# State added on TensorE, the second product in plain fp32, four kb buffers, one decode lane and other TensorE times in the order's model

## The chip, the core and the metric

The kernel runs on one core of one Trainium2 chip. The metric is the device time of one execution in microseconds (us): the median of the runs, 1130.55 us before. A profiled execution gives the trace. Five engines matter: TensorE (PE; its weight loads are PEld), VectorE (DVE), ScalarE (ACT), GpSimd (POOL), and SyncE (SP), which here issues the DMA transfers. Each executes its own instructions in the order in which they were written, and waits at an instruction until what it needs is there.

## The reference

Three layers in a row, in fp32. First a recurrence over 768 steps for 32 pairs of batch and head, each with a 40 x 40 state:

```python
for t in range(S):
    y[:, :, t] = np.einsum('bhd,bhde->bhe', rt, state)
    Sa = np.einsum('bhde,bhe->bhd', state, at)
    state = state * wt[:, :, None, :] - np.einsum('bhd,bhe->bhde', Sa, bt) + np.einsum('bhd,bhe->bhde', vt, kt)
```

Its output, 3072 tokens of 320, goes through a first network (x @ w_in to 1024, h times softmax(h), layer norm times g_ln, @ w_out back to 320) and a second one (@ w_in to 2048, leaky rectifier with alpha, @ w_out to 320). The weights reach the kernel as 64-bit floats, two 32-bit words a value; the kernel turns each into fp32 itself, which is called decoding here.

## The kernel before, in words

**Stages.** The recurrence is done in 24 steps of 32 time steps, called slots (`slot(g)`, lines 1163 to 1210); two slots make a window of 64, four share one triangular inverse. A slot's products on TensorE, each with fp32 operands and results in PSUM: `px` (line 593, the old state and v against a), `pu` (608, the inverse applied), `pf` (633), `pst` (647, the update of the state), `pg` (462 and 686, the products within a chunk), `pss` (667, the new state turned), `py` (718, the output), `pt` (557, kb turned into one of the KBS buffers), and every fourth slot `pv` and `pn` (523, the inverse). They are small, 16 to 104 rows by 16 to 64 columns, and most write to two or four separate column strips of TensorE. Results are copied back to SBUF by ACT, or multiplied or added on the way by DVE: in `stage_st` (lines 640 to 659) DVE adds pst to the old state in VUS and writes the new one (line 652); before the next step ACT copies pss to KBS (671).

**First network.** Three slots behind, a slot's 128 tokens go through `mm1` (767, 16 products of 512 columns), `soft` (785 to 799), `tr1` (826, transposes; ACT casts the result to a short form lnh, line 831, DVE makes the remainder lnl, line 832), `mm2` (842 to 844: for each of 8 row blocks three products of 320 columns, high x high, high x low, low x high, in the reduced fp32r type) and `tr2` (858). x reaches mm1 through DRAM: SP stores Y to xd (751) and loads xt from it (752, 753). From slot 20 on there are no windows left to prepare. The last four groups of tokens are done in phase 2 (lines 1409 to 1414).

**Decode.** Two lanes (`advance`, lines 984 to 1013). A wide one does the first network's 11 pieces of 512 values per partition; a narrow one the second network's 44 pieces of 256, one at a time: SP loads the packed words into the only raw tile (line 923), DVE splits (884, 885), ACT converts (888, 889), DVE sets sign and low bits (892, 896), POOL multiplies (906), SP stores the result to DRAM (1029). The next load is asked for once line 896 of the piece before is done.

**Order.** The program is written out by hand-made planning, at build time. A clock `now` runs along TensorE's instructions: `pace(dt, n)` adds the modelled time of a product and the columns it counts for, `run(engine, cost, f)` the modelled times of the other engines. DVE's background work (scans, masks on a, kb, inverse, decode) is put in by `fill` in a fixed order of priority when the model says that DVE is free. Between the small products, `pace` and `until` take pieces of the first network from a queue, or products whose result nobody reads (`zero`, line 285; `busy`, line 325, in the first four slots), so that TensorE's modelled activity stays above a floor.

**Phase 2** (lines 1297 to 1437) is the second network: products ph (1330) and acc (1348 to 1350), leaky on DVE, casts on ACT and POOL.

Below, the functions that the change touches.

Of the kernel before, what the change touches and what calls it, by code (L numbers as in the profile page):

```python
# [18 lines left out]
D = 40  # L19
# [5 lines left out]
VS, NC, NL = 0, (2, 3, 3, 3), (3, 3, 3, 0)  # L25
# [3 lines left out]
YSV, XSV, YLV, DPV, VRV, W1V = 1, 1, 1, 0, 0, 1  # L29
# [9 lines left out]
WO, JW = 1, 0  # L39
# [6 lines left out]
def tile_kernel(ctx: ExitStack, tc: tile.TileContext, w_fm, a0_fm, a_fm, kb_fm, r_fm, v_fm, v_tm,  # L46
# [19 lines left out]
    lims = flp.tile([128, 2], F32, name="lims")  # L66
    s1 = flp.tile([128, 1], F32, name="s1")
    one = flp.tile([128, 1], F32, name="one")
    bad = flp.tile([1, 1], F32, name="bad")
    badi = flp.tile([1, 1], I32, name="badi")  # L70
    ebias = flp.tile([128, 1], F32, name="ebias")
    half = flp.tile([128, 1], F32, name="half")
    tiny = flp.tile([128, 1], F32, name="tiny")
# [12 lines left out]
    m2 = pool(pm, "m2", 2)  # L86
    b2 = pool(ctx, "b2", 2, side="right")
# [13 lines left out]
    wo1h = cm.tile([128, K1, DM], F32R, name="wo1h")  # L101
    wo1l = cm.tile([128, K1, DM], F32R, name="wo1l")
# [4 lines left out]
    KBP = [ca.tile([128, 1280], F32, name=f"KBS{i}") for i in range(3)]  # L107
# [5 lines left out]
    tri = ca.tile([128, 321], F32, name="tri")  # L113
# [54 lines left out]
    work = {"dec": [], "inv": [], "scan": [], "xs": [], "xm": []}  # L168
    ORDER = {"V": ("inv", "dec", "xm", "scan"), "P": ("xs",)}
    ring, wring, port = [], [], []  # L170
    gens, turns, joins, lanes = [], [], [], []
# [45 lines left out]
    def fill(e):  # L217
        while free[e] < now[0]:
            for s in ("dec",) * (st["slot"] % 4 < 3) + ORDER[e]:
                if work[s] and work[s][0][0]() <= now[0]:  # L220
                    ready, cost, f, done = work[s].pop(0)
                    t = run(e, cost, f, ready())
                    if done:
                        done(t)
                    break
            else:
                return

    def settle():
        if plain():  # L230
            return
        while events and events[0][0] <= now[0]:
            heapq.heappop(events)[2]()
        fill("V")
        fill("P")
        pump()
# [168 lines left out]
    def prep_window(w):  # L405

        for pe in range(2):
            steps = scan_steps(w, pe)
            for i, (cost, f) in enumerate(steps):
                work["scan"].append((lambda: max(at(("wt", w)), at(("yt", 2 * w - 7)) if w > 3 else 0.0), cost, f,  # L410
                                     put(("H", w)) if pe and i == len(steps) - 1 else None))
        for c in range(2):
            for e in range(2):
                work["xm" if XSV else "xs"].append((lambda g=2 * w + c: max(at(("H", w)), at(("a_in", g))) + LAT, (0.7 if XSV else 1.2,),
                                   lambda g=2 * w + c, e=e: mult_a(g, e, 0, 1),
                                   put(("xsh", 2 * w + c)) if e else None))

        def done(t):
            put(("kbf", w))(t)
            if w + 1 < NW:  # L420
                prep_load(w + 1)
                prep_window(w + 1)
        for pe in range(2):
            for i in range(2):
                work["scan"].append((lambda: at(("kb_in", w)), (0.71,), lambda pe=pe, i=i: mult_kb(w, pe, i, nc.vector),
                                     done if pe and i else None))
# [11 lines left out]
    def mult_a(g, e, *pes):  # L438
# [4 lines left out]
        (nc.vector if XSV or w < 2 and e in DA else nc.gpsimd).tensor_tensor(out=o, in0=o, in1=h, op=ALU.mult)  # L443
# [5 lines left out]
    def gen1(g, half):  # L449
# [8 lines left out]
        for p in range(half * 4, half * 4 + 4):  # L458
# [5 lines left out]
            pace(0.19, 188)  # L464
# [26 lines left out]
    def inverse(W):  # L491
# [10 lines left out]
        def step(s):  # L502
            sh = [128, 2, 15 - s, s]
            tmp = b1.tile([128, 256], F32, name="tmp")[:, 0:2 * s * (15 - s)]
# [12 lines left out]
        def low():  # L517
            nc.scalar.activation(out=VR[:, :, 31:15:-1], in_=VT, func=AF.Identity, scale=tri[:, 320:321])

        def units(p, lhsT, rhs, rows, ls):  # L520
            for l in ls:
# [3 lines left out]
                pace(0.042, 16)  # L525
# [24 lines left out]
    def trans(w, q):  # L550
# [4 lines left out]
        for i in range(4):  # L555
            pace(0.09, 150)
            nc.tensor.transpose(pt[:, i, :], kbf[:, q * 4 + i].rearrange("p c a t -> p (c a t)"), ident[0:104, 0:104])  # L557
        for c in range(2):
            k = KBS[(2 * w + c) % 3]
# [25 lines left out]
    def stage_x(g):  # L585
# [3 lines left out]
        for p in range(8):  # L589
# [5 lines left out]
            pace(0.15, 119)  # L595
# [4 lines left out]
    def stage_u(g):  # L600
# [4 lines left out]
        for p in range(8):  # L605
# [3 lines left out]
            pace(0.15, 20)  # L609
# [8 lines left out]
    def blank(p):  # L618
# [3 lines left out]
        note(0.02, 100)  # L622

    def stage_uf(g, pe):
# [4 lines left out]
        for p in range(8):  # L629
# [5 lines left out]
            pace(0.098, 24)  # L635
# [3 lines left out]

    def stage_st(g, pe):  # L640
        k, v, vn = KBS[g % 3], VUS[g % 2], VUS[(g + 1) % 2]
        until(("U", g, pe), ("kb", g))
        p_, bk = bank([128, 8, 40], "pst")
        for p in range(8):
            for e, o in EO:
                q, s = slice(64 * e, 64 * e + 64), pe * 8 + p
                nc.tensor.matmul(p_[o:o + 40, p, :], lhsT=k[q, 1 - e, s, :], rhs=v[q, e, s, :], start=True, stop=True)  # L647
            pace(0.104, 74)
        for e, o in EO:
            sl = slice(pe * 8, pe * 8 + 8)  # L650
            d = vn[o:o + 40, e, sl, :]
            t = run("V", 0.5, lambda d=d, o=o, e=e: nc.vector.tensor_tensor(  # L652
                out=d, in0=p_[o:o + 40], in1=v[o:o + 40, e, sl, :], op=ALU.add), now[0] + PL)
            ring[bk] = t + LAT
            if g % 4 == 3:
                rs = st[(g + 1) // 2]["rs"]
                t = run("V" if VRV else "P", (0.5 if VRV else 0.75,), lambda d=d, o=o: (nc.vector if VRV else nc.gpsimd).tensor_tensor(
# [3 lines left out]
    def stage_s(g, pe):  # L661
        kn, vn = KBS[(g + 1) % 3], VUS[(g + 1) % 2]
        until(("vus", g + 1, pe))
        p_, bk = bank([128, 8, 40], "pss")
        for p in range(8):
# [3 lines left out]
            pace(0.104, 74)  # L669
# [6 lines left out]
    def stage_g2(g, half):  # L676
# [5 lines left out]
        for p in range(half * 4, half * 4 + 4):  # L682
# [4 lines left out]
            pace(0.19, 188)  # L687
        if half == 0:
            return
        def masked(e, q, t):  # L690
            u = run("P", (1.3,), lambda: nc.gpsimd.tensor_tensor(
                out=y[q, e], in0=y[q, e], in1=mask[q].unsqueeze(1).to_broadcast([64, 16, 32]), op=ALU.mult), t)
            put(("ys", g, e))(u + LAT)
        for e in range(2 * YSV):
# [6 lines left out]
        for e in range(0 if YSV else 2):  # L701
            q = slice(64 * e, 64 * e + 64)
            for pe in range(2):
                t = run("A", 0.37, lambda e=e, q=q, pe=pe: nc.scalar.copy(
                    out=y[q, e, pe * 8:pe * 8 + 8], in_=pg[64 * pe:64 * pe + 64, :, e]), now[0] + PL)
            later(t + LAT, lambda e=e, q=q, t=t: masked(e, q, t + LAT))
        ring[bk] = t + LAT

    def stage_y(g):
        w, c = divmod(g, 2)  # L710
        k, y = KBS[g % 3], YS[g % 2]
# [3 lines left out]
        for s in range(16):  # L715
# [3 lines left out]
            pace(0.098, 114)  # L719
# [976 lines left out]
```

## Time and profile before

| what | before |
|---|---|
| median of 3 runs (lowest, highest) | 1130.55 us (1129.92, 1136.22) |
| profiled execution, its span | 1136.73 us, 1134.9 us |
| TensorE busy | 1022.4 us, 90% of the span, 19146 products |
| DVE, ACT, POOL busy | 697.2, 524.6, 290.6 us |
| mean granted clock of TensorE | 0.921 |
| first px of slot 0, of slot 4, of slot 20 | 37.9, 179.5, 658.7 us |

The table is read with care: a busy TensorE may run at 1.2 instead of 2.4 GHz, its fillers count as busy, and the ends of its products are modelled and overlap the next one's start, so that the start-to-start time of a row is the price of a product and not its length. "issue" in the chain is time in which an engine waited for nothing that the profile shows.

### The profile page before, as it was taken

How to read it: one execution, taken by the hardware profiler on the slowest of the kernel's cores; microseconds unless marked ns; L12 is line 12 of the kernel's file. 1: busy time of each engine (PE TensorE's matmuls, PEld its weight loads, DVE VectorE, ACT ScalarE, POOL GpSimd, SP SyncE). 2: the span in 40 equal slices, each digit the busy share in tenths (PEclk: the TensorE clock that was granted, in tenths of full speed). 3: DMA queues.
4: the chain of work that ended last, by engine and by line, in shares of the span. 5: the costliest groups of instructions: out<-in, count | busy, mean ns of one | idle time of the engine just before them, and what ended most of it. 6: DMA issues, size and time to landing. Idle time of an engine off the chain costs nothing.

```text
span 1134.9 us, 43057 instructions
## 1 busy us (share of the span) xinstructions
PE 1022.4 (90%) x19146; PEld 839.8 (74%) x19146; DVE 697.2 (61%) x1372; ACT 524.6 (46%) x1214; POOL 290.6 (26%) x358
## 2 busy tenths in 40 slices
PE   6788879899889879888888899989999999999997
PEld 2455555677677667777776778879899999999997
DVE  8778847787387857894796645555444444444443
ACT  1346434756376536763675467668612121212121
POOL 4401111213112121112111211234333333333332
PEclk8798888989979889986998889999999999999999
DMA  6623334245344333542544343246402020201010
GB/s 172 160 78 109 105 92 105 76 107 146 90 123 125 104 89 93 142 137 54 145 136 118 94 118 94 75 150 192 134 1 70 1 70 1 70 1 48 1 24 15
DMA packets 106757, 104.00 MB, mean 92 GB/s; under 512 B 38340, under 2 KB 85188, under 8 KB 106564
## 3 DMA queue, kind: packets, MB, share of 16 engines
q1 hardware_dynamic: 106564, 101.17, 32.5%
q8 instruction: 152, 2.49, 0.9%
q14 instruction: 41, 0.34, 0.1%
HBM read 75.71 MB, written 25.43 MB: 89 GB/s over the span
## 4 chain that ended last, share of the span: by engine, by line
PE 67%; DVE 14%; DMA 8%; issue 6%; ACT 4%; POOL 1%; SPq 0%; DVEq 0%; ACTq 0%; POOLq 0%
PE ph L1330 15%; PE h L767 7%; PE acc L1350 5%; PE acc L1349 5%; PE acc L1348 5%; PE busy L325 3%; PE pf L633 2%; DMA raw<-in_w_in_dram 2%; PE py L718 2%; PE pss L667 2%; DMA raw<-in_w_out_dram 2%; PE zero L285 2%; PE po L842 2%; PE pst L647 2%; DMA xd<-Y 2%
## 5 line engine op out<-in xcount | busy, mean ns | idle before, releaser
L802 DVE TENSOR_SCALAR gt<-ph,al 128x512 f32<-128x512 f32 (+1 forms) x112 | 75.5, 674 | 188.5 <-PE ph L1330 188.4
L1337 POOL TENSOR_TENSOR gll<-gt,gh 128x512 fp32r<-128x512 f32 (+1 forms) x112 | 129.2, 1154 | 225.5 <-ACT gh L1336 224.2
L1336 ACT CAST gh<-gt 128x512 fp32r<-128x512 f32 (+1 forms) x112 | 62.4, 558 | 249.5 <-DVE gt L803 215.3
L906 POOL TENSOR_TENSOR dec<-em 128x256 f32<-128x256 f32 x44 | 38.5, 876 | 250.4 <-DVE em L896 177.4
L767 PE MATMUL h<-w1h,xt 128*128 128x512 f32 x240 | 97.6, 466 | 1.4 <-ACT h L775 1.3
L1350 PE MATMUL acc<-w2h,gll 128*128 128x320 f32 x288 | 88.9, 309 | 0.0
L1349 PE MATMUL acc<-w2l,gh 128*128 128x320 f32 x288 | 88.9, 309 | 0.0
L1348 PE MATMUL acc<-w2h,gh 128*128 128x320 f32 x288 | 88.8, 308 | 0.0
L325 PE MATMUL busy<-busy 128*128 128x512 bf16 x234 | 70.2, 454 | 5.1 <-DVE busy L1243 3.8
L803 DVE SCALAR_TENSOR_TENSOR gt<-ph,gt 128x512 f32<-128x512 f32 (+1 forms) x112 | 68.8, 615 | 3.7
L842 PE MATMUL po<-wo1h,lnh 128*128 128x320 f32 x192 | 68.2, 355 | 1.2 <-ACT lnh L831 1.2
L767 PE MATMUL h<-w1l,xt 128*128 128x512 f32 x144 | 67.8, 471 | 0.0
L843 PE MATMUL po<-wo1l,lnh 128*128 128x320 f32 x192 | 63.5, 331 | 2.5 <-issue 2.5
L652 DVE TENSOR_TENSOR VUS<-pst,VUS 40x320 f32<-40x320 f32 x92 | 45.0, 489 | 32.9 <-PE pst L647 30.8
L844 PE MATMUL po<-wo1h,lnl 128*128 128x320 f32 x192 | 63.7, 332 | 1.3 <-issue 1.1
L577 POOL MEMSET YS<- 64x512 f32 x44 | 22.9, 521 | 141.3 <-PE py L718 140.1
L561 ACT COPY KBS<-pt 64x160 f32<-64x160 f32 x192 | 54.9, 286 | 9.1 <-PE pt L557 6.6
L1330 PE MATMUL ph<-w1h,w2h 128*128 128x512 f32 x180 | 58.7, 391 | 0.0
L671 ACT COPY KBS<-pss 40x320 f32<-40x320 f32 x92 | 38.6, 420 | 38.1 <-PE pss L667 36.9
L767 PEld LDWEIGHTS h<-w1h,xt 128*128 128x128 f32 x240 | 47.9, 213 | 10.4 <-ACT h L775 2.1
L1348 PEld LDWEIGHTS acc<-w2h,gh 128*128 128x128 f32 x288 | 54.1, 188 | 1.2
L1349 PEld LDWEIGHTS acc<-w2l,gh 128*128 128x128 f32 x288 | 54.1, 188 | 1.2
(197 smaller groups left out, 2556.1 us busy)
## 6 DMA issues: line engine op xcount, KB each, us to landing
kbf<-in_kb_fm_dram SPq DMA_DIRECT2D x24, 416.0 KB
x2d<-x SPq DMA_DIRECT2D x24, 320.0 KB
raw<-in_w_in_dram SPq DMA_DIRECT2D x24, 256.0 KB
xd<-Y SPq DMA_DIRECT2D x24, 256.0 KB
xt<-xd SPq DMA_DIRECT2D x12, 512.0 KB
raw<-in_w_out_dram SPq DMA_DIRECT2D x20, 256.0 KB
wt<-in_w_fm_dram SPq DMA_DIRECT2D x24, 211.7 KB
VUS<-in_v_tm_dram SPq DMA_DIRECT2D x48, 80.0 KB
```

The source lines that it names most:

```text
L325: nc.tensor.matmul(st["busy"], lhsT=busy[:, 0:128], rhs=busy, start=True, stop=True)
L767: nc.tensor.matmul(st["h"][:, ns], lhsT=l, rhs=r, start=j == 0, stop=j == len(ops) - 1)
L802: nc.vector.tensor_scalar(out=tmp, in0=h, scalar1=0.0, scalar2=al, op0=ALU.min, op1=ALU.mult)
L803: nc.vector.scalar_tensor_tensor(out=o, in0=h, scalar=0.0, in1=tmp, op0=ALU.max, op1=ALU.add)
L842: nc.tensor.matmul(po, lhsT=lh[:, k], rhs=wo1h[:, k], start=k == 0, stop=False)
L843: nc.tensor.matmul(po, lhsT=lh[:, k], rhs=wo1l[:, k], start=False, stop=False)
L844: nc.tensor.matmul(po, lhsT=ll[:, k], rhs=wo1h[:, k], start=False, stop=k == K1 - 1)
L1330: nc.tensor.matmul(p, lhsT=l, rhs=r, start=j == 0, stop=j == len(ops) - 1)
L1337: nc.gpsimd.tensor_tensor(out=gll, in0=t, in1=f32(gh), op=ALU.subtract)
L1348: nc.tensor.matmul(acc, lhsT=gh[:, cs], rhs=oh, start=f == 0, stop=False)
L1349: nc.tensor.matmul(acc, lhsT=gh[:, cs], rhs=ol, start=False, stop=False)
L1350: nc.tensor.matmul(acc, lhsT=gll[:, cs], rhs=oh, start=False, stop=f == K2 - 1)
```

## The change

- `stage_st`: a new function `stage_i` first multiplies the old state by the identity into the PSUM banks of pst, and pst is accumulated on top. DVE's add becomes an ACT copy.
- `tr1`, `mm2`: no split of the normed activations and of w_out; one product of plain fp32 per row block instead of three in fp32r.
- KBS has four buffers instead of three; the turns of kb may be placed at point 'a' of a slot instead of 'z'.
- Decode: one lane for both networks, up to two pieces begun and two loaded, with two raw tiles and two work tiles; all pieces up to 512 wide. The scaling of w_out by g_ln goes into the last multiplication. A piece of the second network is decoded into its own raw tile and stored from there.
- `fill`: another order of priority on DVE (inverse first; scan, a and kb ahead of decode once their window is within EARLY = 4 slots).
- Other times and columns in the model of the order for nearly every product; other numbers of pieces per slot.
- Some small tiles are merged or shortened.

```diff
-VS, NC, NL = 0, (2, 3, 3, 3), (3, 3, 3, 0)
+NC, NL = (1, 2, 2, 2), (2, 2, 2, 0)
+EARLY = 4
...
-    KBP = [ca.tile([128, 1280], F32, name=f"KBS{i}") for i in range(3)]
+    KBP = [ca.tile([128, 1280], F32, name=f"KBS{i}") for i in range(4)]
...
     def fill(e):
         while free[e] < now[0]:
-            for s in ("dec",) * (st["slot"] % 4 < 3) + ORDER[e]:
-                if work[s] and work[s][0][0]() <= now[0]:
-                    ready, cost, f, done = work[s].pop(0)
+            soon, passed = ("xm", "kb", "scan"), ()
+            for s in ("inv",) + ("xm", "kb", "scan", "dec", "xm", "kb", "scan"):
+                if work[s] and work[s][0][0]() <= now[0] and (s not in soon or s in passed or
+                                                              st["slot"] >= 2 * work[s][0][4] - EARLY):
+                    ready, cost, f, done, *_ = work[s].pop(0)
...
-            pace(0.19, 188)
+            pace(0.115, 256)
-                pace(0.042, 16)
+                pace(0.072, rows)
-            pace(0.15, 119)
+            pace(0.08, 140)
-            pace(0.15, 20)
+            pace(0.08, 40)
-        note(0.02, 100)
+        note(0.11 * p.shape[1] / 8, 8 * p.shape[1])
...
+    def stage_i(g):
+        v = VUS[g % 2]
+        until(("U", g, 0), ("U", g, 1))
+        st["ps", g] = []
+        for pe in range(2):
+            p_, bk = bank([128, 8, 40], "pst")
+            for e, o in EO:
+                nc.tensor.matmul(p_[o:o + 40], lhsT=ident[0:104 - 8 * e, o:o + 40],
+                                 rhs=v[0:104 - 8 * e, e, pe * 8:pe * 8 + 8, :],
+                                 start=True, stop=False, skip_group_check=True)
+                pace(0.28, 640)
+            st["ps", g].append((p_, bk))
     def stage_st(g, pe):
...
-                nc.tensor.matmul(p_[o:o + 40, p, :], lhsT=k[q, 1 - e, s, :], rhs=v[q, e, s, :], start=True, stop=True)
-            pace(0.104, 74)
+                nc.tensor.matmul(p_[o:o + 40, p, :], lhsT=k[q, 1 - e, s, :], rhs=v[q, e, s, :], start=False,
+                                 stop=p == 7, skip_group_check=True)
+            pace(0.08, 80)
...
-            t = run("V", 0.5, lambda d=d, o=o, e=e: nc.vector.tensor_tensor(
-                out=d, in0=p_[o:o + 40], in1=v[o:o + 40, e, sl, :], op=ALU.add), now[0] + PL)
+            t = run("A", 0.43, lambda d=d, o=o: nc.scalar.copy(out=d, in_=p_[o:o + 40]), now[0] + PL)
...
-        chain(now[0] + PL, [("A", 0.6, lambda: nc.scalar.copy(out=h, in_=pt)),
-                            ("V", 0.7, lambda: nc.vector.tensor_tensor(out=ll[:, 4 * j:4 * j + 4, :], in0=pt,
-                                                                       in1=f32(h), op=ALU.subtract))],
+        u = run("A", 0.6, lambda: nc.scalar.copy(out=st["ln", t][:, 4 * j:4 * j + 4, :], in_=pt), now[0] + PL)
...
-            nc.tensor.matmul(po, lhsT=lh[:, k], rhs=wo1h[:, k], start=k == 0, stop=False)
-            nc.tensor.matmul(po, lhsT=lh[:, k], rhs=wo1l[:, k], start=False, stop=False)
-            nc.tensor.matmul(po, lhsT=ll[:, k], rhs=wo1h[:, k], start=False, stop=k == K1 - 1)
+        nc.tensor.matmul(po, lhsT=st["ln", t][:, piece], rhs=wo1[:, piece], start=piece == 0, stop=piece == K1 - 1)
...
+    def piece(src, dst=None, scales=(), eng="V", end=lambda o: []):
         n = src.shape[1] * src.shape[2]
+        raw = rawp.tile([128, 1024], U32, name="raw")[:, 0:2 * n]
         nc.sync.dma_start(out=raw.rearrange("p (k n) -> p k n", k=src.shape[1]), in_=src.bitcast(U32))
         def steps():
+            em = emp.tile([128, 2, 512], I32, name="em")[:, :, 0:n]
+            o = raw[:, 0:n].bitcast(F32) if dst is None else dst
+            return decode_steps(raw, em[:, 0], em[:, 1], o, scales, eng) + end(o)
...
+    def over():
+        return next((i for i in range(lane["taken"]) if i not in lane["done"]), lane["taken"])
+    def pump():
+        while lane["tasks"] and lane["taken"] < over() + 2:
+            lane["next"].append((lane["tasks"].pop(0)(), now[0] + DMA))
+            lane["taken"] += 1
+        while lane["next"] and lane["due"] > 0 and lane["begun"] < over() + 2:
+            steps, t = lane["next"].pop(0)
...
-                turn(2 * W + 1, q, p(0, 'z'), p(1, 'b'))
+                turn(2 * W + 1, q, p(0, 'a'), p(1, 'b'))
...
-            q.append((0.0, 0, lambda: soft(t1), lambda: decoded(11)))
+            q.append((0.0, 0, lambda: soft(t1), lambda: 0.0))
...
-                q.append((0.4, 960, lambda p=p: mm2(t2, p),
-                          lambda p=p: max(at(("ln", t2, p // 4)), 0.0 if p else wfree())))
+                q.append((0.55, 960, lambda p=p: mm2(t2, p),
+                          lambda p=p: max(at(("ln", t2, p // 4)), 0.0 if p else wfree(),
+                                          decoded(6 + (p * DM + DM + 511) // 512))))
...
         if not fin:
+            stage_i(g)
             stage_st(g, 0)
             stage_st(g, 1)
...
-        if g == 2:
-            until(lambda: decoded(6))
         stage_y(g)
```

## Rows read from the trace of the kernel before

**Rows 1.** Busy time of each engine by stretch: us, busy (instructions), PEclk, DMA, GB/s.
```profile
core 0: us, PE busy (x) PEld busy (x) DVE busy (x) ACT busy (x) POOL busy (x), PEclk, DMA share, GB/s
38.00:180.00 142.00, 117.64 (x3336) 74.63 (x3339) 104.50 (x228) 59.83 (x143) 14.80 (x30) 0.85 0.38 101
180.00:659.00 479.00, 418.50 (x11356) 335.81 (x11349) 350.27 (x746) 279.82 (x687) 94.82 (x148) 0.89 0.42 113
659.00:746.00 87.00, 83.77 (x1949) 69.32 (x1936) 46.57 (x94) 61.71 (x143) 20.43 (x27) 0.97 0.35 92
746.00:810.00 64.00, 59.86 (x383) 55.35 (x382) 33.00 (x57) 47.53 (x98) 23.54 (x25) 0.96 0.57 187
810.00:1135.00 325.00, 316.90 (x1833) 290.74 (x1831) 130.64 (x197) 66.73 (x122) 115.92 (x97) 0.99 0.11 28
```

**Rows 2.** The chain of waits, shares by line: 38 to 180 us, then 180 to 659 us.
```profile
by line: PE busy L325 23.4%; issue 10.0%; PE pv L523 4.5%; PE pf L633 4.4%; PE pn L523 4.0%; DVE XS L482 3.8%; PE pst L647 3.3%; PE pss L667 3.0%; PE pu L608 2.9%; PE h L767 2.8%; DVE VUS L652 2.8%; DVE F L381 2.6%; PE py L718 2.6%; DVE tmp 
...
by line: PE h L767 10.5%; issue 7.7%; DMA raw<-in_w_in_dram 5.5%; DMA raw<-in_w_out_dram 5.2%; PE zero L285 4.5%; DMA xd<-Y 4.2%; PE pss L667 3.5%; PE py L718 3.4%; PE pf L633 3.3%; PE po L842 3.2%; PE ptr L826 2.9%; PE pn L523 2.7%; PE po 
```

**Rows 3.** The chain of waits, pieces from 588 to 622 us: start, us, what.
```profile
592.22 4.88 DMA xd<-Y
...
597.63 6.02 DMA raw<-in_w_in_dram
...
607.01 3.43 DMA raw<-in_w_in_dram
...
616.01 3.51 DMA raw<-in_w_in_dram
```

**Rows 4.** DVE's groups, 180 to 659 us: busy us, mean ns | idle before, releasers.
```profile
L652 DVE TENSOR_TENSOR VUS<-pst,VUS 40x320 f32<-40x320 f32 x64 | 31.3, 489 | 13.6 <-PE pst L647 12.1
...
L832 DVE TENSOR_TENSOR lnl<-ptr,lnh 128x512 fp32r<-128x512 f32 x32 | 21.5, 686 | 17.3 <-ACT lnh L831 17.0
...
L884 DVE TENSOR_SCALAR em<-raw 128x256 int32<-128x256 int32 x39 | 11.9, 306 | 35.0 <-DMA raw<-in_w_out_dram 20.2 <-DMA raw<-in_w_in_dram 14.5
```

**Rows 5.** TensorE's groups, 180 to 659 us, same columns.
```profile
L285 PE MATMUL zero<-D 104*128 104x512 bf16 x127 | 33.8, 396 | 1.9 <-DVE XS L482 1.9
...
L523 PE MATMUL pn<-VR,LMN 32*32 32x32 f32 x1024 | 13.3, 211 | 10.6 <-issue 10.6
L523 PE MATMUL pv<-VT,GR 16*32 16x16 f32 x1024 | 12.6, 192 | 5.9 <-issue 5.9
```

**Rows 6.** TensorE in order of time, around 212 and 616 us: start, us, what.
```profile
210.60 2.07 PE L462 MATMUL pg<-XS,kbf 104*32 104x64 f32 x128
212.65 0.28 PE L608 MATMUL pu<-XP,LMN 32*32 32x40 f32 x8
...
213.40 0.31 PE L842 MATMUL po<-wo1h,lnh 128*128 128x320 f32 x1
...
213.84 0.31 PE L842 MATMUL po<-wo1h,lnh 128*128 128x320 f32 x1
...
616.23 0.80 PE L593 MATMUL px<-VUS,XS 104*32 104x40 f32 x64
616.96 0.41 PE L842 MATMUL po<-wo1h,lnh 128*128 128x320 f32 x1
```

**Rows 7.** What SP's own queue waited for, 180 to 659 us: us, times, longest.
```profile
SPq L923 <- DVE em L896: 36.0, 20, 5.5
...
SPq L752 <- DMA xd<-Y: 25.6, 10, 3.4
```

**Rows 8.** ACT's copies of 40 x 320, 180 to 659 us.
```profile
L671 ACT COPY KBS<-pss 40x320 f32<-40x320 f32 x64 | 26.9, 420 | 19.0 <-PE pss L667 18.2
```

**Rows 9.** The chain of waits over the whole span, a store of a decoded piece.
```profile
253.15 3.95 DMA wd<-dec
```

**Rows 10.** TensorE's fillers, 38 to 180 us.
```profile
L325 PE MATMUL busy<-busy 128*128 128x512 bf16 x174 | 53.2, 457 | 3.8 <-DVE busy L1243 3.8
```

More of the change, by code (lines that the diff above doesn't have):

```diff
@@ L661, in stage_s @@
     def stage_s(g, pe):
-        kn, vn = KBS[(g + 1) % 3], VUS[(g + 1) % 2]
+        kn, vn = KBS[(g + 1) % 4], VUS[(g + 1) % 2]
         until(("vus", g + 1, pe))
@@ L686, in stage_g2 @@
                     nc.tensor.matmul(pg[o:o + 32, p], lhsT=vuf[:, s, i, :], rhs=y[0:104, :, s, :], start=True, stop=True)
-            pace(0.19, 188)
+            pace(0.115, 256)
         if half == 0:
             return
[L690 to L694, printed above, removed]
+        for e in range(2):
             q = slice(64 * e, 64 * e + 64)
@@ L700, in stage_g2 @@
             put(("ys", g, e))(t + LAT)
[L701 to L706, printed above, removed]
         ring[bk] = t + LAT
@@ L975, in chunk_out @@
-            return steps
-        return ([lambda j=j: chunk_in(j) for j in range(6)] +
-                [lambda c=c: chunk_out(*c) for c in cuts(K1 * DM, WO)])
-    def pump():
-        for lane in lanes:
-            advance(lane)
-    def advance(q):
-        i = q["taken"]
-        if q["tasks"] and not q["next"] and q["read"] and q["done"] >= (6 if i == 6 else i - 1):
-            q["next"] = q["tasks"].pop(0)(), now[0] + DMA
-            q["taken"] += 1
-        if q["due"] <= 0 or not q["next"] or q["busy"]:
-            return
-        q["busy"], q["read"] = True, False
-        q["due"] -= 1
-        get, t = q["next"]
-        q["next"] = None
-        s, end = get()
-        def read(u):
-            q["read"] = True
-            chain(u, s[-1:], over)
-        def over(u):
-            if q["wide"]:
-                q["busy"], q["free"] = False, u
-            chain(u, end, ended)
-        def ended(u):
-            q["done"] += 1
-            if q["wide"] and q["done"] == 6 and "moved" in st:
-                moved()
-            if not q["wide"]:
-                q["busy"], q["free"] = False, u
-        chain(max(t, q["free"]), s[:-1], read)
@@ L1170, in due @@
         def due(n):
[L1171 removed]
+            lane["due"] += n
         if g + 1 < NG:
@@ L1261, in phase1 @@
                 slot(g)
-            lanes[1]["due"] = 100
-            while events or any(q["busy"] or q["next"] or q["tasks"] for q in lanes) or any(work.values()):
+            lane["due"] = 100
+            while events or lane["next"] or lane["tasks"] or any(work.values()):
                 now[0] += 0.1
@@ L1587, in tile_kernel @@
             ms.enter_context(tc.manual_schedule(engines={mybir.EngineType.PE}))
-        for t in (w1_tasks(), w2_tasks()):
-            lanes.append({"tasks": t, "due": 0 if lanes else len(t), "next": None, "busy": False, "free": 0.0, "done": 0,
-                          "taken": 0, "read": True, "wide": not lanes})
+        lane["tasks"] = w1_tasks() + w2_tasks()
+        lane["due"] = 11
         phase1()
```

202 lines of the change are left out of this document (85 added, 117 removed).

## The prediction

> **What bounds the kernel now.** I read the busy table by stretch first. The last 325 us, the second network alone, keep TensorE busy for 316.90 us at 0.99 of its clock [rows 1]; no part of the change touches them, and I carry them over unchanged. The change lives in the recurrence, from 38 to 746 us, and in the 64 us behind it. In the middle stretch, 180 to 659 us (slots 4 to 19, 479/16 = 29.9 us a slot), no engine is full: DVE is busy for 350.27 us (73%), ACT for 279.82 (58%). TensorE shows 418.50 us (87%), but a good part of that is not needed work: 33.8 us are zero products that only keep its clock up [rows 5], and the granted clock is 0.89, that is, a fifth of the time at 1.2 GHz instead of 2.4, or up to 0.11 x 479 = 53 us of full clock. From 659 to 746 us TensorE really is full: 83.77 of 87 us, clock 0.97.
>
> So the middle is bound by waits, and the chain of waits says which. Of the chain from 180 to 659 us, 5.5% + 5.2% = 10.7% (51 us) are loads of packed weights into raw; 4.2% (20 us) are the store xd<-Y; 7.7% are issue [rows 2]. The reader should see how a weight decode that nothing needs soon can hold up everything: a load of 3.43 to 6.02 us lies on the chain [rows 3], DVE executes in its written order, and so the split of line 884 stands on DVE waiting for its load, for 35.0 us in all [rows 4], with the masks, Yt and lnl behind it, for which TensorE waits. In the first stretch, 38 to 180 us, 23.4% of the chain are fillers (busy), and DVE is busy for 104.50 of 142 us [rows 1, 2].
>
> **Plain fp32 second product.** It replaces three reduced-precision products of 320 columns, which start 213.84 - 213.40 = 0.44 us apart as a group, 0.147 each, by one fp32 product [rows 6]. Fp32 appears in the trace as two records for each product (64 records for the 32 products of a px). The lowest price is one pass per record, 2 x 0.147 = 0.29 us. For the other end, px needs 616.96 - 616.23 = 0.73 us for 64 records of 40 columns, 11.4 ns each; at the 0.46 ns a column of the 0.147 us product 40 columns would need 18 ns, so its four column strips run side by side. Then the 128 records (64 products of 64 columns, four at a time) of pg, 212.65 - 210.60 = 2.05 us, are 1024 columns, 2.0 ns each: 0.64 us for 320 columns. I take 0.60, because pg is the same kind of product. There are 192: 192 x (0.60 - 0.44) = +31 us of TensorE; the ends are 192 x (0.29 - 0.44) = -29 and 192 x (0.64 - 0.44) = +38.
>
> On this price the Trainium skill, page "FP8 and Floating Point Precision", section "TensorE Precision Notes", speaks against the change: true fp32 takes four passes through the array, not the two that a count of records suggests. By that rule an estimate from the row of 0.147 us is 192 x (4 x 0.147 - 0.44) = +28 us, by two passes it would be -29; the rate of pg agrees with the rule.
>
> What leaves DVE for it: 48 subtractions lnl, in the middle 21.5 us of work and 17.3 us in which DVE stood waiting for ACT ahead of them [rows 4].
>
> **State by an identity product.** Each of 46 calls gets two fp32 products of 320 columns, on different column strips: 0.60 us if they run side by side, as those of px do, 1.20 if not. I take 0.60: 46 x 0.60 = +28 us (upper end 55). They come behind the wait for U and in front of pst, so they lengthen that path by 1.2 us a slot; px, pss and py of the slot follow. In exchange 92 adds of 489 ns go from DVE to ACT [rows 4], where a copy of the same shape takes 420 ns [rows 8]: +38.6 us on ACT. ACT has 199 us free in the middle, but its queue is in order too: the new copies stand behind the two copies to VUF, and pss and the copies to KBS wait for them.
>
> **Decode in one lane, two buffers.** 44 pieces of 256 columns become 28 (16 of 512, 12 of 256), still 28 x up to four DVE instructions; the columns are the same, so I count DVE's decode time at nothing either way (work on DVE that has 27% free covers a difference). What counts is the load. Before, one raw tile serves: its load cannot be issued until line 896 of the piece before has read it, SP itself stands 36.0 us for that [rows 7], and the piece asked for next runs at once. Now two tiles exist, and a load is issued as soon as the piece two before has ended; with two pieces or one a slot that is about half a slot, 15 us, ahead of use, against the 6.02 us of the slowest load. I therefore let most of the 35.0 us on DVE go. Of the 51 us on the chain I credit 30: what is late next is xd<-Y with the SP queue, and TensorE itself.
>
> The price on SP: the decoded piece now lies in its own raw tile, so the next load into it waits until the store to wd has landed, 3.95 us [rows 9]. For 28 pieces that is some 28 x 4 = 112 us in which SP stands, and the loads of VUS, YS, VUF, wt and the xt loads stand behind it. SP waits 36.0 us for line 896 and 25.6 us for xd already [rows 7]. I cost this at nothing because those loads are issued a slot ahead; without that cover it is the second rival.
>
> **Four kb buffers, priorities, times in the model.** A fourth buffer lets the turns of kb be placed without waiting for the last y. No instruction is added. The order's model now charges a unit of pv and pn 0.072 us instead of 0.042, so it puts more of the large products between them. This matters: TensorE stands 10.6 + 5.9 = 16.5 us there for nothing but issue [rows 5]. I credit 14 of the clock's 53 and these 16.5 together; the ends are 0 and 40.
>
> **The sum**, against the profiled execution of 1136.7 us (span 1134.9 and 1.8 around it):
> - 38 to 180 us: 16 adds, 7.8 us, leave DVE, and the five pieces of w_out lose a scaling and a subtraction; the identities (4 x 1.2 us) lie inside the 53.2 us of fillers [rows 10]. -4.
> - 180 to 659 us: loads -30; adds and lnl, 84 us of DVE's work and standing [rows 4], mostly covered, -8; clock and issue -14; TensorE +16 x 1.2 = 19 and +128 x 0.16 = 20, of which I charge 16 because 33.8 us of zero products and 479 - 418.5 = 60.5 us of idle time can take the rest. -36.
> - 659 to 746 us: TensorE is full, so 3 x 1.2 + 32 x 0.16 = +9.
> - 746 to 810 us: 32 x 0.16 = +5, all on the path.
>
> Together -26: 1110.7 for an execution like the profiled one. The median of the runs is 1130.55, 6.2 below that; so I forecast 1130.55 - 26 = 1104.5, in round numbers **1105 us**, its own range 1085 to 1119.
>
> **The rivals.**
> 1. TensorE becomes the bound, and it is slower. Place: slots 4 to 19 and the full slots behind. None of the +39 us there finds cover, because the idle time sits ahead of products (behind ACT's copies, behind issue) where the order cannot put anything; the 14 of the full stretches come on top: 53. Of the loads only 20 are won: +33, **1163 us**. It decides once less than half of the added 2.4 us a slot replaces fillers or idle time. For it: a fully loaded TensorE from 659 us on. Against: 94 us of fillers and idle time in the middle. Chance 0.20.
> 2. SP's queue takes back what raw gave. The stores' landings hold SP, xd and xt arrive later, and the first network's products wait. If 8 of the 28 holds hit that path at 4 us each, 30 us are lost again: +4, **1135 us**. For it: xd<-Y is already 20 us of the chain. Against: most loads are a slot ahead. Chance 0.23.
> 3. It gains more: with DVE no longer standing, and TensorE's true times in the order, idle time and low clock fall together. A slot goes from 29.9 to 26 us: -62, with -4 and +14 that is -52, **1078 us**. For it: the four slots from 659 to 746 us, where nothing but TensorE bounds, take 87/4 = 21.8 us each. Against: issue and the clock are no waits that the change removes. If the fp32 product has two passes, another 20 or so are possible. Chance 0.15.
>
> **How the numbers follow.** The forecast has 0.42. About 1%, 11 us, is what a measurement of this kernel tells from no change. Forecast and rival 3 are faster: 0.57; rival 2 is the same: 0.23; rival 1 is slower: 0.20. The range 1062 to 1146 takes the forecast, rival 2, most of rival 3 and the lower part of rival 1; the ends of the fp32 price (-29 to +38, half of it covered) lie in it.
>
> **What would show it.** Right: next to no wait of line 884's successor for raw, under 10 us; raw gone from the chain of the middle; slots 4 to 19 below 28 us; 384 records of po about 0.30 us apart, so 0.60 a product; pst no longer on DVE; clock above 0.89 and fewer zero products in the middle. Wrong: a middle stretch as long as before with SP waiting on wd (rival 2), or with TensorE near 95% busy and the tail longer by 14 us (rival 1). The forecast falls if raw was only the last of several waits that end together, so that taking it away moves nothing.

## The result, and the profile after

The changed kernel took 1146.6 us (median of 4 runs, 1141.1 to 1150.15) against 1130.86 us of the kernel before on the same chip: ratio 1.0121, 95% interval [1.0072, 1.0169]. Run again, 12 times beside 23 runs of before: 1144.95 us, ratio 1.0072 [1.0044, 1.0101]. It is slower by 0.7 to 1.2 per cent where 2.3 per cent faster (1105 us) was forecast; the range ended at 1146. Below, ratios are to the kernel before on the same chip, and 1.0072 is what the edits of the changed kernel are held against.

Stretches of the profiled execution (1150.15 us, span 1148.4), cut at the first px of slots 0, 4 and 20 and where slot 23 and the tail end:

```profile
core 0: us, PE busy (x) PEld busy (x) DVE busy (x) ACT busy (x) POOL busy (x), PEclk, DMA share, GB/s
38.40:169.60 131.20, 108.80 (x3289) 72.51 (x3292) 87.35 (x189) 61.00 (x149) 15.56 (x31) 0.84 0.36 98
169.60:663.40 493.80, 444.38 (x11347) 321.27 (x11345) 304.58 (x614) 305.43 (x731) 94.93 (x132) 0.91 0.42 114
663.40:756.70 93.30, 89.51 (x1949) 66.13 (x1946) 33.82 (x59) 62.84 (x145) 18.44 (x24) 1.00 0.30 78
756.70:820.00 63.30, 60.36 (x346) 52.01 (x345) 28.18 (x49) 47.64 (x99) 24.36 (x25) 0.97 0.58 190
820.00:1148.40 328.40, 320.60 (x1837) 291.86 (x1835) 130.78 (x196) 66.34 (x123) 115.92 (x97) 0.99 0.10 28
```

Against [rows 1], with before cut at the same first px (37.9, 179.5, 658.7, 746.2 us): the first stretch is 10.4 us shorter, slots 4 to 19 are 14.6 longer (493.8 for 479.2), slots 20 to 23 are 5.8 longer and all behind them 3.0. The whole loss is made in slots 4 to 19, where a gain of 36 was forecast. DVE lost 46 us of work there as meant, ACT gained 26; TensorE is busy for 26 us more and still idle for 49.

DVE's groups in slots 4 to 19, answering [rows 4]:

```profile
L713 DVE TENSOR_TENSOR YS<-pg,mask 64x256 f32<-64x256 f32 x64 | 27.0, 422 | 34.1 <-PE pg L706 33.2
...
L881 DVE TENSOR_SCALAR em<-raw 128x512 int32<-128x512 int32 (+1 forms) x30 | 12.8, 426 | 54.5 <-DMA raw<-in_w_in_dram 34.2 <-DMA raw<-in_w_out_dram 20.1
```

The wait for raw (line 881 is line 884 of before) should have gone; it rose from 35.0 to 54.5 us. In one piece of the chain of waits all its consequences are seen (start, us, what):

```profile
425.45 1.40 PE pst L667 x64
426.85 0.30 SPq L586
...
427.73 5.26 DMA raw<-in_w_in_dram
...
433.08 0.44 DVE em L881
...
433.54 0.72 ACT em L885
434.26 0.52 ACT em L886
434.78 1.13 ACT P L803
...
435.94 0.42 ACT VUS L673
...
436.37 0.43 ACT VUS L673
...
436.84 1.94 PE pg L468 x64
```

The same place, TensorE, then SP's own queue, in order of time:

```profile
430.68 0.61 PE L771 MATMUL h<-w1h,xt 128*128 128x512 f32 x2
436.84 1.94 PE L468 MATMUL pg<-XS,kbf 104*32 104x64 f32 x64 [5.55 <-ACT VUS L673]
```

```profile
420.23 0.84 SPq L951 DMA_DIRECT2D od<-raw  x2
426.82 0.80 SPq L586 DMA_DIRECT2D VUS<-in_v_tm_dram  x2
427.73 0.95 SPq L916 DMA_DIRECT2D raw<-in_w_in_dram  x2
```

Two pieces are stored out of both raw tiles; then SP stands at a load of VUS that waits for pst, and both tiles are loaded again behind it. DVE stands for it, then ACT's em, then the two VUS copies that the change put on ACT, and TensorE stands 5.55 us. A weight that nothing needs soon holds the recurrence, as before the change. Of the eleven loads that make up the 54.5 us, seven (31.3 us) waited last for the store out of their own tile to land; four (23.1 us), this one among them, had no wait of their own and came behind another transfer on SP. And TensorE pays a second time, for it comes back at half clock:

```profile
431.30:436.80 5.50, 0.00 (x0) 0.00 (x0) 3.63 (x8) 3.21 (x5) 0.10 (x1) 0.93 0.21 68
436.80:445.00 8.20, 8.16 (x141) 6.80 (x143) 6.07 (x15) 4.69 (x12) 2.16 (x1) 0.50 0.46 138
```

After 5.5 us without a product the granted clock is 0.50 (1.2 of 2.4 GHz) for the next 8 us. SP's waits, 170 to 663 us, answering [rows 7]:

```profile
SPq L586 <- PE pst L667: 78.5, 13, 11.7
SPq L951 <- POOL raw L902: 52.3, 18, 9.8
...
SPq L916 <- DMA wd<-raw: 14.9, 11, 2.5
SPq L916 <- DMA od<-raw: 12.0, 4, 5.4
```

### The profile page after: what moved, and what is told of

Its sections match the earlier page's. It is cut to its first block, busy times and chain, and to the rows that moved or that the text cites. A ratio compares the mean times of both kernels' runs of the same rounds, so it can differ in the third digit from the quotient of the medians.

```text
span 1148.4 us, 42660 instructions
## 1 busy us (share of the span) xinstructions
PE 1049.8 (91%) x19078; PEld 818.5 (71%) x19078; DVE 615.7 (54%) x1150; ACT 553.0 (48%) x1269; POOL 298.6 (26%) x352
## 4 chain that ended last, share of the span: by engine, by line
PE 75%; DMA 7%; issue 5%; ACT 5%; DVE 3%; POOL 1%; SPq 1%; POOLq 0%; DVEq 0%; ACTq 0%
PE ph L1274 15%; PE po L841 9%; PE h L771 7%; PE acc L1292 5%; PE acc L1293 5%; PE acc L1294 5%; PE pf L639 3%; PE pss L687 3%; PE py L728 3%; PE zero L286 2%; PE pst L667 2%; PE busy L326 2%; DMA raw<-in_w_in_dram 2%; PE pst L654 2%; PE pg L706 2%
## 5 line engine op out<-in xcount | busy, mean ns | idle before, releaser
L841 PE MATMUL po<-wo,ln 128*128 128x320 f32 x384 | 133.1, 484 | 2.4 <-ACT ln L833 1.7
L841 PEld LDWEIGHTS po<-wo,ln 128*128 128x128 f32 x384 | 74.5, 207 | 30.6 <-issue 7.1
L583 POOL MEMSET YS<- 64x512 f32 x44 | 23.1, 524 | 228.7 <-PE py L728 227.5
L902 POOL TENSOR_TENSOR raw<-em 128x512 f32<-128x512 f32 (+1 forms) x28 | 42.6, 1527 | 122.4 <-DVE em L893 77.7
L713 DVE TENSOR_TENSOR YS<-pg,mask 64x256 f32<-64x256 f32 x96 | 40.5, 422 | 57.1 <-PE pg L706 55.5
L786 POOL TENSOR_TENSOR sm<-sm,const 128x1 f32<-128x1 f32 x24 | 14.2, 590 | 165.0 <-ACT sm L783 165.0
L1294 PEld LDWEIGHTS acc<-w2h,gll 128*128 128x128 f32 x288 | 54.1, 188 | 0.0
L881 DVE TENSOR_SCALAR em<-raw 128x512 int32<-128x512 int32 (+1 forms) x39 | 17.8, 456 | 67.1 <-DMA raw<-in_w_in_dram 46.2
```

Source lines behind the costliest of these rows:

```text
L841: nc.tensor.matmul(po, lhsT=st["ln", t][:, piece], rhs=wo1[:, piece], start=piece == 0, stop=piece == K1 - 1)
L902: (nc.vector if eng == "V" else nc.gpsimd).tensor_tensor(out=o, in0=f32(m), in1=f32(e), op=ALU.mult)
L1294: nc.tensor.matmul(acc, lhsT=gll[:, cs], rhs=oh, start=False, stop=f == K2 - 1)
```

## The experiments

**The prices on TensorE, with the order of the instructions kept.** In these three TensorE executes the same list but for the edited products (in a_three and a_one some instructions of ACT and DVE behind 730 us change places). a_noid takes the identity products out (their modelled time stays):

```diff
-                nc.tensor.matmul(p_[o:o + 40], lhsT=ident[0:104 - 8 * e, o:o + 40],
-                                 rhs=v[0:104 - 8 * e, e, pe * 8:pe * 8 + 8, :],
-                                 start=True, stop=False, skip_group_check=True)
...
-                nc.tensor.matmul(p_[o:o + 40, p, :], lhsT=k[q, 1 - e, s, :], rhs=v[q, e, s, :], start=False,
-                                 stop=p == 7, skip_group_check=True)
+                nc.tensor.matmul(p_[o:o + 40, p, :], lhsT=k[q, 1 - e, s, :], rhs=v[q, e, s, :], start=True, stop=True)
```

> The kernel after without the identity products, the model's time for them kept, so that the order of the rest stays (the old state is left out of the update). It takes 46 x 0.54 = 25 us of work off TensorE, on the path from U to pst. Theory P: 17 to 25 us less than after, 1122 to 1130 us. Theory W: at most 8 us less, 1138 us or more.

1121.85 us, 0.988 [0.9791, 0.9968]: 1.9 per cent below the changed kernel, some 22 us (the interval alone leaves 12 to 32) for 46 x 0.54 = 25 us of products. By the middle figure they were hardly covered; the interval leaves it open whether half of them were.

a_three makes the fp32 product three fp32r products of the same operands; a_one a single one (the first hunk, and the same for ln, without the last):

```diff
-    wo1 = cm.tile([128, K1, DM], F32, name="wo1")
+    wo1 = cm.tile([128, K1, DM], F32R, name="wo1")
...
-        nc.tensor.matmul(po, lhsT=st["ln", t][:, piece], rhs=wo1[:, piece], start=piece == 0, stop=piece == K1 - 1)
+        for i in range(3):
+            nc.tensor.matmul(po, lhsT=st["ln", t][:, piece], rhs=wo1[:, piece], start=piece == 0 and i == 0,
+                             stop=piece == K1 - 1 and i == 2)
```

> The kernel after, with three fp32r products of the same operands in place of the one plain fp32 product (their sum is three times the product, remainders left out): TensorE's price of before, 0.44 us instead of 0.54, 192 x 0.10 = 19 us less work, same order. Theory P: 13 to 19 us less than after, 1127 to 1134 us, the time of before. Theory W: at most 6 us less, 1140 us or more.

> The kernel after, with the second product of the first network as one fp32r product instead of plain fp32, the order on TensorE unchanged (the remainders of both operands are left out). It takes 192 x (0.54 - 0.15) = 75 us of work off TensorE. Theory P (TensorE's own work in the written order sets the pace of the recurrence): 50 to 75 us less than after, 1070 to 1097 us. Theory W (the waits of DVE and SP for loads and stores set it, and work on TensorE falls into idle time): at most 25 us less, above 1120 us.

a_three: 1134.17 us, 0.9965 [0.9927, 1.0004], some 12 us below the changed kernel for 192 x (0.54 - 0.44) = 19 us less of products. a_one: 1138.6 us, 1.0025 [0.9986, 1.0065], only some 5 us below, although 192 x (0.54 - 0.147) = 75 us of products are gone. Its slots 4 to 19 show where they went:

```profile
165.60:649.30 483.70, 414.64 (x11229) 309.89 (x11230) 304.77 (x614) 304.18 (x730) 96.21 (x132) 0.86 0.42 116
```

TensorE is busy for only 30 us less than in the changed kernel, at a granted clock of 0.86 instead of 0.91, and idle for 69 us instead of 49. Here work taken out of a stretch that waits bound turned into idle time, and the granted clock fell with it. Theory P of this expectation (50 to 75 us less) failed. And a_three, which takes away a quarter as much, gained no less (8 to 16 us by its interval, a_one 1 to 10): in this order a product's price on the whole does not follow from its length.

**Is it the stores?** a_dec decodes a piece into its work tile, so that no load waits for a store; the orders of TensorE, DVE and ACT stay.

```diff
-            o = raw[:, 0:n].bitcast(F32) if dst is None else dst
+            o = dst if dst is not None else (f32(em[:, 0]) if eng == "P" else raw[:, 0:n].bitcast(F32))
```

> The kernel after, with a piece of the second network decoded into its work tile instead of its raw tile; TensorE's, DVE's and ACT's orders are the same. The next load into a raw tile then waits for no store (SP stood 26.9 us for these stores between 170 and 663 us). Theory W in the form of the second rival (SP held by the stores): 10 us or more less than after, under 1137 us, and DVE's wait for raw falls from 54.5 to under 25 us. Theory P: within 5 us of after, 1142 to 1152 us, whatever DVE's wait does.

1136.58 us, 1.0074 [1.0025, 1.0123]: no difference by the ratios. DVE's wait for raw in slots 4 to 19 fell from 54.5 to 33.6 us, not under 25 as theory W said, and the time did not follow:

```profile
L881 DVE TENSOR_SCALAR em<-raw 128x512 int32<-128x512 int32 (+1 forms) x30 | 12.5, 418 | 33.6 <-DMA raw<-in_w_in_dram 18.2 <-DMA raw<-in_w_out_dram 14.4 <-POOL em L902 0.8
```

The loads' waits for stores, 14.9 + 12.0 us, are gone, but the load now waits for the reader, as in before:

```profile
SPq L586 <- PE pst L667: 70.4, 13, 13.7
...
SPq L916 <- DVE em L893: 18.9, 6, 7.4
```

**Is it that two pieces in work hold both tiles?** a_beg1 begins a piece only when the one before has ended.

```diff
-        while lane["next"] and lane["due"] > 0 and lane["begun"] < over() + 2:
+        while lane["next"] and lane["due"] > 0 and lane["begun"] < over() + 1:
```

> The changed kernel with one number altered: a piece of weights is begun only when the one before it has ended, so that of the two raw tiles one is always free for the load ahead. Theory A (the load is late because two pieces may be in work at once, and then hold both tiles; the third load waits until one of them has ended and is needed at once): DVE's wait for raw falls from about 65 us in the whole run to below 30 us, and the time falls from 1146 to 1125 to 1135 us. Rival B (the load is late because SP stands in front of it, at load_g or at the landing of a store): the wait for raw stays between 50 and 70 us and the time within 6 us of the changed kernel's.

1123.68 us, 0.9905 [0.9869, 0.9941]. DVE's wait for raw in the whole run, which was 67.1 us in the changed kernel:

```profile
L881 DVE TENSOR_SCALAR em<-raw 128x512 int32<-128x512 int32 (+1 forms) x39 | 16.1, 413 | 1.9 <-DMA raw<-in_w_out_dram 1.0 <-DMA raw<-in_w_in_dram 0.5
```

and its slots 4 to 19:

```profile
175.90:636.90 461.00, 427.07 (x11326) 310.83 (x11317) 298.96 (x602) 304.22 (x731) 91.34 (x132) 0.94 0.43 119
```

The wait is gone: theory A of this expectation. But SP stands less as well, at line 586 for 34.9 us instead of 78.5 in these slots:

```profile
SPq L586 <- PE pst L667: 34.9, 10, 5.4
```

So this run alone does not rule rival B out. Two runs below speak against it: a_paces, with two pieces in work, stands at line 586 for 27.4 us in the whole run (a_beg1 58.4) and still waits 36.7 us for raw; and in a_kb3beg1 the same edit takes the wait of a_kb3 from 57.5 to 11.9 us. TensorE is idle for 34 us instead of 49 and busy for 427 instead of 444 at a higher clock.

**The same idea in the kernel before.** b_raw2 gives the narrow lane a second raw tile and loads into it as soon as a piece begins, one piece in work (small tiles are merged to make room).

```diff
-            raw = m1.tile([128, 512], U32, name="raw2")
+            raw = m1.tile([128, 512], U32, name="raw2", bufs=2)
...
-        if q["tasks"] and not q["next"] and q["read"] and q["done"] >= (6 if i == 6 else i - 1):
+        if q["tasks"] and not q["next"] and (q["read"] or not q["wide"]) and q["done"] >= (6 if i == 6 else i - 1):
```

> The kernel before with a second raw tile in the narrow decode lane (and some small tiles merged to make room): the next load is issued as soon as a piece begins, not when it has been read. The forecast's claim (loads of raw hold up the recurrence, 51 us of its chain): 20 us or more less, 0.982 of before or less, and DVE's wait for raw falls from 40.8 to under 15 us. Theory S (several waits end together, TensorE's stream paces): 0.994 to 1.006, whatever DVE's wait does.

1119.18 us, **0.9827 [0.9792, 0.9862]**. DVE's wait for raw in the narrow lane falls from 40.8 us in the whole run to 11.8:

```profile
L882 DVE TENSOR_SCALAR em<-raw 128x256 int32<-128x256 int32 x44 | 14.0, 319 | 11.8 <-DMA raw<-in_w_in_dram 6.4 <-POOL dec L904 3.3 <-DMA raw<-in_w_out_dram 1.5
```

**The fourth kb buffer and the point of the turns.** a_kb4z goes back to point 'z' (the first hunk, and the same for the next slot's turns), a_kb3 to three buffers as well, and a_kb3beg1 is a_kb3 with a_beg1's edit.

```diff
-                turn(2 * W + 1, q, p(0, 'a'), p(1, 'b'))
+                turn(2 * W + 1, q, p(0, 'z'), p(1, 'b'))
...
-    KBP = [ca.tile([128, 1280], F32, name=f"KBS{i}") for i in range(4)]
+    KBP = [ca.tile([128, 1280], F32, name=f"KBS{i}") for i in range(3)]
```

> The kernel after with three kb buffers and the turns of kb at point 'z' again. If the fourth buffer brought a good part of what the change gained beside its new work: 10 us or more above after, 1.020 of before or more. If not: 1.005 to 1.017, as after.

> The changed kernel with four kb buffers kept and the turns of kb placed at point 'z' of a slot as before. If the cost of this part is that the turns are put ahead of the first products of a slot (their place in the order), the time is that of three buffers, 1125 to 1132 us. If the cost hangs on the fourth buffer itself (what the planner does with the freedom it gives, whatever the point), the time stays at 1141 to 1150 us.

> The changed kernel with both: three kb buffers with the turns at point 'z', as before, and one piece of weights begun at a time. If the two causes add up (about 18 us for the buffers as measured, 10 to 20 for the loads), the time is 1108 to 1118 us, below the kernel before by 1 to 2 per cent. If they share one cause, the time is 1122 to 1130 us, that of three buffers alone.

a_kb3: 1128.31 us, 0.9913 [0.9879, 0.9946]. a_kb4z: 1125.63 us, 0.9939 [0.9905, 0.9973]; so the buffer itself shows no cost. But a_kb3beg1: 1135.62 us, 1.0031 [0.9988, 1.0073]. Its wait for raw is 11.9 us:

```profile
L881 DVE TENSOR_SCALAR em<-raw 128x512 int32<-128x512 int32 (+1 forms) x39 | 16.6, 426 | 11.9 <-DMA raw<-in_w_in_dram 11.7
```

Two edits that seemed to be worth 1.6 and 1.7 per cent are worth 0.4 together; seen from a_kb3, beginning one piece at a time cost 1.2 per cent although it took 46 us of waiting for raw away. They cannot both be gains of that size that add up.

**What a new order alone does.** Every edit that moves a modelled time or a due time makes the planner write all the orders anew. a_null (identity product of the changed kernel, the first hunk) and b_null (pst of the kernel before, the second) do that and nothing else.

```diff
-                pace(0.28, 640)
+                pace(0.27, 640)
...
-            pace(0.104, 74)
+            pace(0.102, 74)
```

> The changed kernel with the modelled time of the identity product 0.27 instead of 0.28 us (nothing else): a change of no meaning that only makes the planner write the order out anew. Theory A (the gains of 14 to 24 us measured against the changed kernel come from what each edit does): the time stays within 6 us of the changed kernel's 1145 us. Rival B (the order of the changed kernel is a poor draw, and any edit that redraws it lands on average near 1130 us): the time is 1125 to 1137 us, and what single edits of the changed kernel showed below about 1.5 per cent is not told apart from a redraw.

> The kernel before with the modelled time of a pst product 0.102 instead of 0.104 us (nothing else): the same test on the order of the kernel before. If its order is an ordinary draw, the time is 1125 to 1140 us; if it was a lucky one, 1140 to 1155 us, and the change would then not be slower in itself; the second raw tile's gain of 1.7 per cent stands against the same spread.

a_null: 1136.67 us, 1.0014 [0.9982, 1.0046]. b_null: 1152.99 us, **1.0154 [1.0106, 1.0202]**, more than the whole change cost, from 0.002 us in the model. b_null's slots 4 to 19 take 490.4 us instead of 479.2, and its wait for raw is 55.8 us instead of 40.8:

```profile
176.60:667.00 490.40, 425.76 (x11345) 339.69 (x11340) 347.60 (x748) 279.33 (x688) 94.06 (x149) 0.87 0.41 110
```

```profile
L884 DVE TENSOR_SCALAR em<-raw 128x256 int32<-128x256 int32 x44 | 13.2, 301 | 55.8 <-DMA raw<-in_w_out_dram 33.8 <-DMA raw<-in_w_in_dram 21.7
```

a_null is the changed kernel in another order; its slots 4 to 19 take 473.1 us:

```profile
169.70:642.80 473.10, 433.80 (x11361) 313.81 (x11351) 306.47 (x616) 306.05 (x733) 92.87 (x132) 0.94 0.42 118
```

Against the changed kernel (493.80) 10.6 us are TensorE busy at a higher clock and 10.1 us are idle time, half and half. These are two single executions, of 1150.15 and 1132.33 us; a_null's own lie between 1130.0 and 1143.3, and by the ratios the two kernels are only 0.6 per cent (7 us) apart. A difference between two profiles is coarser than one between medians.

**Parts alone, and the model's times.** b_id is before with the identity product and ACT copy (stage_i and stage_st of the change), b_fp32 before with the plain fp32 product (no lnl, no low half of w_out, 0.55 us in the model), a_dve the changed kernel with DVE's add and no identity product, b_paces before with the new modelled times, a_paces after with the old ones, a_same the changed kernel once more.

> The kernel before with one part of the change alone: the state added by the identity product, copied by ACT. Theory P: +25 us of TensorE's work come on the path in full, less a little for DVE's 45 us: 1.012 to 1.025 of before. Rival D: DVE's relief pays for it, 0.995 to 1.005.

> The kernel before with one part of the change alone: the second product of the first network in plain fp32 (0.55 us a piece in the model), without lnl and without the low half of w_out. Theory P (TensorE's own work counts in full): +192 x 0.10 = 19 us, 1.012 to 1.017 of before. Rival D (DVE's relief, 48 subtractions lnl and the standing ahead of them, pays for it): 0.990 to 1.004.

> The kernel after with the state added by DVE as before (no identity products, no time for them in the model, the order planned anew), all else as after. Theory P: the identity's 25 us of TensorE's work go, and DVE, which has room, takes 92 adds (45 us of its time) at no cost: 15 to 27 us less than after, 0.988 to 0.998 of the kernel before. Rival D (DVE's adds cost as much on the way as the identity did): within 5 us of after, 1.008 to 1.017 of before.

> The kernel before with the new times and columns of TensorE in the order's model alone (three products of a piece at 0.44 us instead of 0.40). If the gain that the change brought beside its new work on TensorE (some 30 us) came from the times: 0.970 to 0.985 of before. If it came from DVE's relief and the decode lane: 0.990 to 1.010.

> The kernel after with the old times and columns in the order's model (those of the identity and of the plain fp32 product stay). If the times brought the gain: 20 us or more above after, 1.030 of before or more. If not: within 8 us of after, 1.005 to 1.020 of before.

> The kernel after once more, unchanged, as the measure for the others on this chip: 1.007 to 1.017 of before.

| kernel | us | ratio [95%] |
|---|---|---|
| b_id | 1135.07 | 1.0030 [0.9997, 1.0063] |
| b_fp32 | 1134.8 | 0.9990 [0.9960, 1.0021] |
| a_dve | 1138.15 | 1.0018 [0.9976, 1.0061] |
| b_paces | 1129.29 | 0.9986 [0.9946, 1.0027] |
| a_paces | 1143.38 | 1.0060 [1.0021, 1.0099] |
| a_same | 1144.95 | 1.0072 [1.0044, 1.0101] |

All redraw the order (a_same aside), so none tells more than that neither part alone, nor the modelled times, moves before by more than a redraw does. In a_paces DVE's wait for raw is 36.7 us in the whole run, where a_same has 64.4, and the ratio is nearly the same:

```profile
L881 DVE TENSOR_SCALAR em<-raw 128x512 int32<-128x512 int32 (+1 forms) x39 | 15.0, 384 | 36.7 <-DMA raw<-in_w_in_dram 28.1 <-POOL YS L583 4.2 <-DMA raw<-in_w_out_dram 4.2
```

**Both useful parts together.** b_raw2fp32 is b_raw2 with b_fp32's edit (no diff beyond those two).

> The kernel before with a second raw tile in the narrow lane whose load is issued when a piece begins, and with the second product of the first network in plain fp32 (no split of the activations and of w_out). If the two add up, the time is 1112 to 1120 us: fp32 alone gave 0.999 and the second tile 0.983. If DVE, freed of the split, was covered by the standing for raw, then with that gone the shorter DVE queue gives more: 1100 to 1111 us. If TensorE now decides, its 192 x 0.10 us more (a product takes 0.54 against 0.44) show: 1121 to 1135 us.

1106.21 us, **0.9777 [0.9723, 0.9831]**: the fastest version, below both kernels. Its slots 4 to 19:

```profile
177.20:618.20 441.00, 401.98 (x11192) 303.12 (x11186) 327.14 (x720) 281.10 (x694) 104.68 (x151) 0.94 0.45 123
```

## Why the prediction was wrong

**The failed step: the load.** The prediction said that with two tiles "a load is issued as soon as the piece two before has ended; with two pieces or one a slot that is about half a slot, 15 us, ahead of use", let "most of the 35.0 us on DVE go" and credited 30. The rule was read rightly, but not what it does beside the other one: the lane also begins two pieces, so both tiles can be in work, and the piece two before ends when the next is wanted. Of the eleven loads that DVE stood for, ten were issued 2.8 to 6.3 us ahead of use (427.73 for 433.08 in the piece shown). Measured: 54.5 us instead of next to none. That two pieces in work are the cause of this wait is shown: with one, on the same two tiles and with SP's waits for stores no shorter (31.7 us for 26.9), it is 1.9 us in the whole run of a_beg1 and 11.9 in a_kb3beg1; with two it is 36.7 to 69.9 us in all other versions of the changed kernel.

What the wait costs in time is less clear, and this is the second thing that the credit had wrong. In before, raw did bound, as the prediction read it: b_raw2 lies 1.7 per cent below before, and both versions with a second tile (0.9827, 0.9777) lie below all five without it (0.9986 to 1.0154). But that is some 20 us (16 to 24), not 30. In the changed kernel it stays open: a_beg1 gained 1.7 per cent, of which the wait's part and the new order's are not told apart (a_null got 0.6 by the order alone), a_kb3beg1 lost 1.2 against a_kb3, and a_paces, with 28 us less of the wait, gained nothing. The prediction's own last sign, that raw is one of several waits that end together, is not excluded there. Without the 30 the sum is -26 + 30 = +4, a forecast of 1135 us.

**What the sum left out: the order.** It priced each edit against a fixed order, but the planner writes a new one for any edit. Three orders of before that differ in modelled times alone (before, b_null, b_paces) stand at 1.0000, 1.0154, 0.9986; three of the changed kernel (a_same, a_null, a_paces) at 1.0072, 1.0014, 1.0060. The means are 1.0047 and 1.0049. So the 0.7 to 1.2 per cent are a fact of this program, but these draws do not show that the change itself costs anything; with three of each, which differ by 1.7 and 0.6 per cent among themselves, a cost or gain of up to about 2 per cent stays open. The corrected +4 us (1.004) agrees with that mean, which with so few draws is no proof of it.

**TensorE's work: the price was near, its cover is open.** An fp32 product takes 0.54 us at full clock (I took 0.60, its records start 0.269 apart), a pair of identity products 0.54 (0.60). I charged 16 + 9 + 5 = 30 us for what was not covered; a_noid and a_three give 22 + 12 = 34 (by their intervals 12 to 32 and 8 to 16) of 25 + 19 = 44 us of work. By these two, rival 1 was right that this work finds next to no cover. But a_one, with the same list on TensorE, took 75 us away and gained 5, and b_id and b_fp32, which put the two parts into before in new orders and relieve DVE, cost no more than a redraw. So rival 1's mechanism is not shown, and TensorE is busy for 90% of slots 4 to 19, not near the 95% that it named. Slots 20 to 23 gave +5.8 where +9 was said, the rest +3.0 for +5.

**Clock and issue, credited with 14.** The clock of slots 4 to 19 rose from 0.89 to 0.91, and issue at pv and pn fell from 16.5 to 13.1 us; fillers did not fall (34.8 us for 33.8). In a_null half of what the order gained was clock, beside less idle time, and in a_one more idle time went with a lower clock. So I would no longer price the clock as a term of its own.

**Rival 2, the stores.** Its 1135 us was the nearest number, but not by its mechanism: the stores held SP's loads of raw for 26.9 us, not 112, and a_dec took that away without a gain in time. What they held up was the next load of raw itself, which the prediction saw waiting for them and still put 15 us ahead of use.

**Four kb buffers, at nothing.** a_kb3 and a_kb4z lie 1.6 and 1.3 per cent below the changed kernel, which is more than its own redraws show (0.6) and less than before's (1.7). a_kb3beg1 speaks against a cause. Whether the earlier point costs anything stays open. The first stretch gained 10.4 us where 4 was said; none of the runs takes that apart.

## What to carry to other kernels

Two buffers load ahead only if at most one of them is in work: count what may be begun against what may be loaded, not the tiles. Where a planner writes the order, redraw it by a meaningless change of one modelled time before an effect of 1 or 2 per cent is put down to an edit, and take prices from edits that keep the order. Here a wait that idled TensorE cost twice, once as idle time and once as the half clock behind it.

## What was not expected of the hardware

The fp32 product of 128 x 320 has two prices within one execution. Four of them (8 records) in the chain of the changed kernel:

```profile
210.15 4.36 PE po L841 x8
...
240.51 2.37 PE po L841 x8
```

and the granted clock there, in the column behind POOL:

```profile
210.15:214.51 4.36, 4.36 (x9) 2.60 (x9) 1.71 (x4) 0.00 (x0) 0.00 (x0) 0.54 0.21 50
240.51:242.88 2.37, 2.37 (x13) 1.46 (x12) 2.06 (x3) 2.29 (x7) 0.22 (x1) 1.00 0.08 18
```

1.09 us a product at 0.54, 0.59 at 1.00 (0.54 from one start to the next): a price taken from a stretch at full clock is not the price in a stretch that waits. Ahead of the first, from 205 to 208 us, TensorE was busy for 0.65 of 3 us.
